# Row sums of the softmax weights with 128 moving columns instead of 4, in a recurrence followed by a soft mixture of experts

## The chip, the cores and the metric

The kernel runs on one core of one Trainium2 chip. The metric is the device time of one execution in microseconds; the figure given for a kernel is the median of several executions. A profile of one further execution shows what each engine did: TensorE (PE for its matmuls, PEld for its weight loads), VectorE (DVE), ScalarE (ACT), GpSimd (POOL) and SyncE (SP), which here only issues transfers.

## The reference

```
def _attn_ref(x, f_logit, lower_bound):          # 4 sequences of 5056 tokens, 256 channels
    sig = 1.0 / (1.0 + np.exp(-f_logit))
    f = lower_bound + (1.0 - lower_bound) * sig
    i = 1.0 - f
    for t in range(S):
        h = f[:, t] * h + i[:, t] * x[:, t]
        y[:, t] = h

def _moe_ref(x, phi, w1, w2):                    # all 20224 tokens; 8 experts of 4 slots, F = 1024
    logits = x @ phi                             # 32 slots
    d = softmax of logits over the tokens
    slot_input = d.T @ x
    for e in range(E):
        h = np.maximum(slot_input[e] @ w1[e], 0.0)
        slot_out[e] = h @ w2[e]
    c = softmax of logits over the slots
    return c @ slot_out
```

The output is 20224 x 256 in float32, 20.7 MB. The change is about the denominators of `c`: for each token the sum of its 32 exponentials.

## The kernel before

There are three stages.

*Recurrence.* Tokens come in 10 groups of 512 for each of the 4 sequences, 40 units in all. SyncE issues the loads of `x` and `f_logit`, ScalarE computes the gates, TensorE turns them to channels on partitions, VectorE runs the scans, TensorE turns the result back and multiplies it with `phi`. ScalarE writes the exponentials to `etall`, which stays on chip: 128 partitions (4 sequences x 32 slots) by 5056 tokens, bf16. The sums over the tokens, `slot_ps`, gather in PSUM along the way. GpSimd issues the loads of the expert weights (`load_w`); the last expert's `w2` comes in three parts.

*Experts.* After the last unit all is one chain on TensorE: slot inputs (L596), first layer (L624), transposes of its result (L639), second layer of the first four experts (L660) and then of the last four (L670), eight matmuls of 128x128 weights and 256 columns for each expert. Between those eight-matmul pieces lie the row sums: after the first of the four experts `row_sums(0)` with 16 matmuls, after the second `row_sums(1)` and `row_sums(2)` with 16 and 7, one small matmul for the 64 tokens left over (L393), and `SPINS = 7` matmuls whose results nobody reads (`spin`, L151, 256 columns each). The last two experts follow, then four more spins. VectorE takes the reciprocals of the sums (L677, L683, L684) into `rrow`, and scales the second layer's result to `slot_out` (L686); GpSimd makes `slot_bd` from it (L688).

*Output.* For every 128 tokens a matmul of the exponentials with `slot_out` (L705, one sequence, 32 weight rows) or `slot_bd` (L755, two sequences, 64 weight rows) gives the weighted sum, VectorE or ScalarE scales it by `rrow` while moving it out of PSUM (L695, L699 and L760, L766), and SyncE issues the store (L727 for the first 2 MB in small pieces, L769, L743, L786 afterwards).

The instruction order on each engine is the order of the program text. `row_sums` takes 128 tokens at a time as the weights of a matmul: the column `ew[:, :, r]` is a view of `etall` with a step of 16 elements (7 in the last block). The moving operand is `ones`, 128 partitions by 4 columns, column b being one on the 32 partitions of sequence b. So the result is 128 tokens by 4 sequences, and it goes to 4 neighbouring float32 columns of `rs_ps`, which is a view of the first half (one bank of 512 columns) of the PSUM tile `tail`. The second half of `tail` takes the spins' results. Columns 256 to 319 of the first half held the slot inputs, which were read long before.

Of the kernel before, what the change touches and what calls it, by code (L numbers as in the profile page):

```python
# [10 lines left out]
BF16 = mybir.dt.bfloat16  # L11
# [7 lines left out]
def kernel(  # L19
# [10 lines left out]
    nc = tc.nc  # L30
    B, S, D = x.shape
# [4 lines left out]
    P = 128  # L36
    DC = D // P
    FC = F // P
    R = 4
    G = P * R  # L40
    n_grp = (S + G - 1) // G
# [25 lines left out]
    consts = ctx.enter_context(tc.tile_pool(name="consts", bufs=1))  # L67
# [16 lines left out]
    def rep_constants(b):  # L84
        blk = ident_f[ds(b * NS, NS), ds(b * NS, NS)]
        nc.gpsimd.tensor_copy(rep[ds(b * NS, NS)], blk.unsqueeze(1).broadcast_to([NS, B, NS]))

    ones = consts.tile([P, B], BF16, name="ones")
    nc.vector.memset(ones, 0.0)
    for b in range(B):  # L90
        nc.vector.memset(ones[ds(b * NS, NS), ds(b, 1)], 1.0)

# [69 lines left out]
    with tc.tile_pool(name="sp2", bufs=3) as sp2, \  # L162
# [24 lines left out]
        def long(n):  # L187
            return 2 * B <= n < n_unit - 2 * B
# [38 lines left out]
        def gate(n, k=2):  # L227
            if n % 2 == 0:
                sts[n // 2] = sp2.tile([P, 2, R, D], BF16, name="s_t", tag="s_t")
            s_t, f_t = sts[n // 2][:, ds(n % 2, k)], fs[n // 2][:, ds(n % 2, k)]  # L230
            if n // B == odd:
                m = (R + R3) * D
                s_t = s_t.rearrange("p u r d -> p (u r d)")[:, :m]
                f_t = f_t.rearrange("p u r d -> p (u r d)")[:, :m]
            nc.scalar.activation(s_t, f_t, ACT.Sigmoid, scale=-1.0)  # L235
# [33 lines left out]
        def s_to_channels(n):  # L269
            if n % 2 == 0:  # L270
                pss[n // 2] = psp.tile([P, 2, P, R], F32, name="sp", tag="sp")
            to_channels(n, pss[n // 2][:, n % 2], sts[n // 2][:, n % 2],
                        sts[n // 2][:, 0, R3])
# [12 lines left out]
        def decay(n, k=2, os=range(DC)):  # L286
            T = used(n // B)
            sp = pss[n // 2].rearrange("c u p r -> c u (p r)").bitcast(BF16)
            if long(n):
                sp = sp.rearrange("c u (p r o) -> c p u r o", r=R, o=DC)  # L290
                for o in os:
                    decays[n // 2, o] = apool.tile([P, 2, G], F32, name="a", tag=f"a{o}")
                    a = decays[n // 2, o].rearrange("c u t -> c (u t)").rearrange(
                        "c (p u r) -> c p u r", u=2, r=R)
                    nc.scalar.activation(a, sp[:, :, :, :, o], ACT.Identity,  # L295
                                         scale=nomlb[:, ds(o, 1)], bias=1.0)
                return
            sp = sp.rearrange("c u (t o) -> c u t o", o=DC)
            for o in os:
                if n % 2 == 0:  # L300
                    decays[n // 2, o] = apool.tile([P, 2, G], F32, name="a", tag=f"a{o}")
                nc.scalar.activation(decays[n // 2, o][:, ds(n % 2, k), :T],  # L302
                                     sp[:, ds(n % 2, k), :T, o], ACT.Identity,
                                     scale=nomlb[:, ds(o, 1)], bias=1.0)
# [57 lines left out]
        def exps(g):  # L362
            gs = batch_of(g)
            if g == gs[-1]:
                T = sum(rows(i) for i in gs) * R
                nc.scalar.activation(etall[:, ds(first(gs[0]), T)], lgs[0][:, :T], ACT.Exp,
                                     accum_out=csum[:, ds(g, 1)])
# [16 lines left out]
                ets[k] = et[:, i]  # L384

        def row_sums(i):
            t0, n_r = blocks[i]
            ew = etall[:, ds(t0, P * n_r)].rearrange("s (p r) -> s p r", r=n_r)
            for r in range(n_r):
                nc.tensor.matmul(rs_ps[:, t0 // P + r], ew[:, :, r], ones,  # L390
                                 start=True, stop=True, skip_group_check=True)
            if i == len(blocks) - 1:
                nc.tensor.matmul(rs_ps[:, n_grp * R - 1, ds(0, B // 2)],  # L393
                                 left.rearrange("s t u -> s (t u)"), pair_ones,
                                 start=True, stop=True, skip_group_check=True)
# [17 lines left out]
        def unit(f, m):  # L413
            if 0 <= m < n_unit:
                f(m)
# [64 lines left out]
        for n in range(n_unit):  # L480
            if n < SINGLE - 2:
                if n:
                    unit(to_tokens, n - 1)
                    unit(u_to_channels, n + 1)
                s_to_channels(n + 2)
                if n + 3 < SINGLE:
                    gate(n + 3, 1)
                decay(n + 2, 1)
                if n + 3 == SINGLE:
                    gate(n + 3)  # L490
                if n % 2 == 0:
                    unit(load, n + AHEAD)
                unit(enter, n + 3)
                rep_constants(n)
            else:
                end = n >= n_unit - 6
                if n % 2 == 0:
                    unit(load, n + AHEAD)
                    if n == SINGLE - 2:
                        to_tokens(n - 1)  # L500
                        keep_tokens(n - 1)
                    if not end and n >= SETTLED:
                        unit(gate, n + 4)
                else:
                    unit(decay, n + 1)
                    if n < SETTLED:
                        gate(n + 3)
                    if n == n_unit - 5:
                        gate(n + 3)
                        exps(odd - 1)  # L510
                if not end and n != n_unit - 7:
                    group(exps, n - 2)

                unit(enter, n + 3)
                for _ in range(W_AT.get(n, 0)):
                    load_w(w_next[0])
                    w_next[0] += 1

                if n == n_unit - 2:
                    unit(u_to_channels, n + 1)  # L520
                if n != SINGLE - 2:
                    unit(to_tokens, n - 1)
                if n == n_unit - 2:
                    keep_tokens(n - 1)
                if n % 2 == 0:
                    unit(s_to_channels, n + 2)
                    unit(s_to_channels, n + 3)
                if n != n_unit - 2:
                    unit(u_to_channels, n + 1)
                if n in (n_unit - 5, n_unit - 4):  # L530
                    idle(2)
                elif n == SINGLE - 2:
                    idle(1, True)
                elif n < n_unit - 4 and n % (2 * B) in (1, 5, 6, 7):
                    idle(2 if n in (6, 7) else 1)
                if n == n_unit - 2:
                    tail = psp.tile([P, 2, G], F32, name="tail", tag="sp")
                    rs_ps = tail[:, 0, ds(0, n_grp * R * B)].rearrange(
                        "p (q b) -> p q b", b=B)
                    late_ps, odd_ps = (  # L540
                        tail[:, 1].bitcast(BF16)[:, ds(i * R * P, R * P)].rearrange(
                            "p (r s) -> p r s", r=R) for i in range(2))
                    logits(odd)
                    exps(odd)
                    slots(odd - 1)
                    spin(tail[:, 1], 1, G)
                    odd_weights()
                elif not end and long(n - 1):
                    if n % B == 0:
                        g = (n - 1) // (2 * B) * 2  # L550
                        for i in range(2):
                            logits(g + i, [2, 3] if n % (2 * B) == 0 else [0, 1])
                elif not end:
                    group(logits, n - 1)
            if n == n_unit - 1:
                logits(last, [0, 1, 2])
                late_exps([0, 1, 2])
                idle(1)
                late_weights([0, 1, 2], nc.scalar.copy)

            unit(scan, n)
            if n not in (SINGLE - 2, n_unit - 2):
                unit(keep_tokens, n - 1)
            if n == n_unit - 3:
                weights_to_tokens(odd - 1)
                slots(odd - 2)
            elif not n >= n_unit - 6:
                group(weights_to_tokens, n - 3)
                batch(slots, n - 4, 0)
                batch(slots, n - 4, 1)  # L570
                if n > 2 * B and n % (2 * B) == 3:
                    idle(1)
# [254 lines left out]
```

## Time and profile before

| | |
|---|---|
| median of 3 runs | 198.8 us (198.79 to 198.85) |
| the profiled execution | 199.45 us, of which the span shown is 197.7 us |
| PE, DVE, ACT, POOL busy | 78%, 73%, 70%, 52% of the span |
| mean granted TensorE clock | 0.862 |
| moved by DMA | 70.75 MB, mean 358 GB/s |
| recurrence, experts, output | to about 128 us, to 144.5 us, to 195 us |

The page cuts the span into 40 slices of 4.94 us. Its digits are tenths; PEclk is the clock that TensorE was granted, in tenths of full speed:

```profile
PE   0688599888989979897979888999969999960000
...
PEclk9999979999999999999999999999696555555555
DMA  5999999999999999999999999999639999999995
```

Slice 28 (counted from 0) begins at 138 us. Times in all other views count from the start of the span; a line such as "136.66 0.93 PE tail L390 x16" in the chain of waits says that from 136.66 us on, for 0.93 us, sixteen matmuls of line 390 into the tile `tail` were the work that everything behind them waited for.

### The profile page before, as it was taken

To read this page: it belongs to the slowest core of one execution; us is meant where nothing else is said; L and a number is where in the kernel's file an instruction comes from. 1 tells how busy PE (TensorE), PEld (TensorE's weight loads), DVE (VectorE), ACT (ScalarE), POOL (GpSimd) and SP (SyncE) were. 2 spreads that over 40 slices of the span, in tenths; PEclk is the share of its full clock that TensorE was granted. 3 is DMA by queue.
4 is the path that set the end of the run, shared out by engine and by line. 5 is a ranking of instruction groups with operands and counts; after the bars stand their busy time and mean duration, and the time that the engine had idled before them with its cause. 6 is when DMAs were issued, how large, how long until landed. Compare 5 with 4: busy or idle time off the path is not lost.

```text
span 197.7 us, 3232 instructions
## 1 busy us (share of the span) xinstructions
PE 153.2 (78%) x1198; PEld 107.1 (54%) x1198; DVE 143.6 (73%) x165; ACT 137.4 (70%) x193; POOL 103.1 (52%) x78
## 2 busy tenths in 40 slices
PE   0688599888989979897979888999969999960000
PEld 0477468675766758675766676558753533310000
DVE  2669779999899999999999999343168877850000
ACT  3588678899699998899996794621057889990000
POOL 2689586884998488895979886390030000000000
PEclk9999979999999999999999999999696555555555
DMA  5999999999999999999999999999639999999995
GB/s 209 417 420 422 427 431 423 428 426 347 390 426 428 380 356 423 426 409 306 411 421 354 264 219 213 215 212 212 107 119 423 419 421 424 428 458 438 424 424 215
DMA packets 14161, 70.75 MB, mean 358 GB/s; under 512 B 1585, under 2 KB 2866, under 8 KB 10178
## 3 DMA queue, kind: packets, MB, share of 16 engines
q1 hardware_dynamic: 11520, 62.13, 75.9%
q0 software_dynamic: 2624, 8.42, 21.4%
q8 instruction: 9, 0.15, 0.3%
q14 instruction: 6, 0.05, 0.1%
q10 hardware_dynamic: 2, 0.00, 0.0%
HBM read 58.23 MB, written 20.71 MB: 399 GB/s over the span
## 4 chain that ended last, share of the span: by engine, by line
PE 37%; DVE 23%; DMA 14%; POOL 6%; ACT 5%; issue 4%; SPq 0%; ACTq 0%; DVEq 0%; POOLq 0%
DVE h L313 16%; DMA x_t<-in_x_dram 14%; PE op L755 12%; POOL u_t L246 6%; DVE ht L343 4%; PE hp L326 3%; PE up L267 3%; PE so_ps L670 2%; PE sp L261 2%; PE op L705 2%; PE lg L357 2%; PE tail L151 2%; DVE ob L695 1%; PE slot_ps L407 1%; PE slot_ps L183 1%
## 5 line engine op out<-in xcount | busy, mean ns | idle before, releaser
L246 POOL TENSOR_TENSOR u_t<-s_t,x_t 128x1024 bf16<-128x1024 bf16 (+1 forms) x39 | 82.4, 2128 | 22.5 <-ACT s_t L235 14.0
L313 DVE TENSOR_TENSOR_SCAN h<-a,h,up 128x512 bf16<-128x512 f32 (+1 forms) x72 | 86.9, 1252 | 3.5 <-PE up L267 1.9
L235 ACT ACTIVATE s_t<-f_t 128x2048 bf16<-128x2048 f32 (+2 forms) x23 | 38.3, 1668 | 6.8 <-DMA f_t<-in_f_logit_dram 6.8
L326 PE MATMUL hp<-ident_f,h 128*128 128x128 f32 (+1 forms) x160 | 29.3, 308 | 7.7 <-DVE ht L343 5.9
L326 PEld LDWEIGHTS hp<-ident_f,h 128*128 128x128 f32 (+1 forms) x160 | 23.3, 207 | 17.9 <-DVE ht L343 11.3
L261 PE MATMUL sp<-ident_f,s_t 128*128 128x128 f32 x144 | 21.8, 296 | 6.3 <-ACT s_t L235 4.4
L295 ACT ACTIVATE a<-sp,lbs 128x1024 f32<-128x1024 bf16 x24 | 25.4, 1115 | 0.6 <-PE sp L261 0.6
L755 PE MATMUL op<-slot_bd,etall 64*128 64x512 bf16 x62 | 24.1, 594 | 1.7 <-DVE ob L695 1.4
L766 ACT ACTIVATE oc<-op,rrow 128x256 f32<-128x256 f32 x60 | 22.7, 489 | 2.8 <-PE op L755 2.3
L760 DVE TENSOR_TENSOR oc<-op,rrow 128x1024 f32<-128x1024 f32 x16 | 19.2, 1222 | 5.3 <-PE op L755 5.3
L261 PEld LDWEIGHTS sp<-ident_f,s_t 128*128 128x128 f32 x144 | 17.5, 151 | 8.2 <-ACT s_t L235 5.3
L302 ACT ACTIVATE a<-sp,lbs 128x512 f32<-128x512 bf16 (+2 forms) x22 | 17.8, 858 | 4.2 <-PE sp L261 3.8
L267 PE MATMUL up<-ident_f,u_t 64*128 64x64 f32 x192 | 17.8, 230 | 2.0 <-POOL u_t L246 1.8
L183 PE MATMUL slot_ps<-rep,ident_f 128*128 128x256 f32 x54 | 17.7, 423 | 0.1
L755 PEld LDWEIGHTS <-etall 64*128 64x128 bf16 x62 | 8.9, 154 | 15.5 <-issue 11.7
L267 PEld LDWEIGHTS up<-ident_f,u_t 64*128 64x128 f32 x192 | 14.0, 138 | 6.0 <-POOL u_t L246 2.5
L343 DVE COPY ht<-hp 128x512 f32<-128x512 f32 (+1 forms) x22 | 14.7, 669 | 1.2 <-PE hp L326 1.2
L343 ACT COPY ht<-hp 128x512 f32<-128x512 f32 (+1 forms) x18 | 10.5, 581 | 6.7 <-PE hp L326 6.7
L699 ACT ACTIVATE ob<-op,rrow 128x256 f32<-128x256 f32 x15 | 5.8, 477 | 10.9 <-PE op L705 10.7
L313 DVE TENSOR_TENSOR_SCAN h<-a,up 128x512 bf16<-128x512 f32 x8 | 9.3, 1209 | 2.6 <-ACT a L302 1.8
L261 PE MATMUL up<-ident_f,u_t 128*128 128x128 f32 x48 | 9.8, 338 | 0.7 <-POOL u_t L246 0.7
L183 PEld LDWEIGHTS slot_ps<-rep,ident_f 128*128 128x128 f32 x54 | 8.6, 193 | 2.5 <-issue 1.1
(107 smaller groups left out, 152.5 us busy)
## 6 DMA issues: line engine op xcount, KB each, us to landing
f_t<-in_f_logit_dram SPq DMA_DIRECT2D x12, 1024.0 KB, 12.5
x_t<-in_x_dram SPq DMA_DIRECT2D x12, 1024.0 KB, 12.1
out_dram<-oc SPq DMA_DIRECT2D x6, 2048.0 KB, 11.1
w_sb<-in_moe_w_dram POOLq DMA_DIRECT2D x14, 512.0 KB, 10.9
f_t<-in_f_logit_dram SPq DMA_DIRECT2D x12, 512.0 KB, 8.4
x_t<-in_x_dram SPq DMA_DIRECT2D x12, 512.0 KB, 9.9
out_dram<-oc SPq DMA_DIRECT2D x4, 896.0 KB, 5.2
out_dram<-ob SPq DMA_DIRECT2D x1, 2048.0 KB, 8.2
```

The source lines that it names most:

```text
L183: nc.tensor.matmul(slot_bank[:, 1], ident_f, wide_rep, start=False, stop=False, skip_group_check=True)
L235: nc.scalar.activation(s_t, f_t, ACT.Sigmoid, scale=-1.0)
L246: nc.gpsimd.tensor_tensor(uts[n][:, :r], s_t[:, :r], x_t[:, :r], ALU.mult)
L261: nc.tensor.transpose(ps[:, :, r], t[:, r], ident_f)
L267: nc.tensor.transpose(v[:, :, r], t(r)[k].bitcast(F32), ident_f[k, k])
L295: nc.scalar.activation(a, sp[:, :, :, :, o], ACT.Identity, scale=nomlb[:, ds(o, 1)], bias=1.0)
L313: nc.vector.tensor_tensor_scan(h[:, :T, o], decays[n // 2, o][:, n % 2, :T], up[:, :T, o], hs[number(g - 1, b)][:, ds(used(g - 1) - 1, 1), ...
L326: nc.tensor.transpose(hp[:n_p, r], hw[:, :n_p, r], ident_f)
L343: copy(hts[g][:n_p, b].rearrange("p r d -> p (r d)").bitcast(F32), hps.pop(n)[:n_p].rearrange("p r c -> p (r c)"))
L755: nc.tensor.matmul(op[:, i_r].rearrange("p u d -> p (u d)"), ew[:, :, r + i_r], slot_bd[ds(j * 2 * NS, 2 * NS)].rearrange("s u d -> s (u d)"),
L760: nc.vector.tensor_tensor(ob[:, :, ds(r, k)].rearrange("p u r d -> p r u d"), op[:, ds(0, k)], scale[:, ds(r, k)].unsqueeze(3).broadcast_t ...
L766: nc.scalar.activation(ob[:, u, r + i_r], op[:, i_r, u], ACT.Copy, scale=scale[:, r + i_r, ds(u, 1)])
```

## The change

`ones` becomes 128 x 128. Its first four columns are as before, the other 124 are ones. Each of the 39 matmuls of `row_sums` streams all 128 columns and so writes 128 float32 columns, from the column at which its own four begin. The next matmul, four columns further, overwrites all but the first four of these, and so on; what lies to the right of the last matmul's four columns is read by nobody. The line numbers below `ones` move by one; the blank line in `row_sums` moves those behind it by another, and `sums` by a third.

```
-    ones = consts.tile([P, B], BF16, name="ones")
-    nc.vector.memset(ones, 0.0)
+    ones = consts.tile([P, P], BF16, name="ones")
+    nc.vector.memset(ones, 1.0)
+    nc.vector.memset(ones[:, ds(0, B)], 0.0)
     for b in range(B):
         nc.vector.memset(ones[ds(b * NS, NS), ds(b, 1)], 1.0)
...
         def row_sums(i):
+
             t0, n_r = blocks[i]
             ew = etall[:, ds(t0, P * n_r)].rearrange("s (p r) -> s p r", r=n_r)
             for r in range(n_r):
-                nc.tensor.matmul(rs_ps[:, t0 // P + r], ew[:, :, r], ones,
+                nc.tensor.matmul(sums[:, ds((t0 // P + r) * B, P)], ew[:, :, r], ones,
                                  start=True, stop=True, skip_group_check=True)
...
                     tail = psp.tile([P, 2, G], F32, name="tail", tag="sp")
-                    rs_ps = tail[:, 0, ds(0, n_grp * R * B)].rearrange(
+                    sums = tail[:, 0]
+                    rs_ps = sums[:, ds(0, n_grp * R * B)].rearrange(
                         "p (q b) -> p q b", b=B)
```

## The prediction

> **What bounds the kernel now.** I read the shares of the page first, then the chain of waits of the last third, then the granted clock in stretches, then the start of the output stage. Two stages matter. From 148 us on the output transfers set the time: the DMA share is about 1 until 195 us (0.92 to 1.22 over stretches of 2 us), at about 425 GB/s for 20.7 MB, while the last computing instruction ends at 178 us. So whatever brings the first output forward brings the end forward, as long as the transfers then stay fed. Before that, between the last scan and the first output, the weights for the output are a chain of TensorE work without a gap. Its pieces (start, length, both in us, engine, tile, line, count):
>
> ```profile
> 136.23 0.43 PE so_ps L674 x2
> 136.66 0.93 PE tail L390 x16
> 137.60 0.89 PE so_ps L670 x8
> 138.49 1.30 PE tail L390 x23
> 139.79 0.03 PE tail L393
> 139.82 1.42 PE tail L151 x7
> 141.24 2.79 PE so_ps L670 x16
> 144.03 0.03 issue
> 144.06 0.49 DVE slot_out L686
> ```
>
> The 39 row sums (L390) are on the path: 58 ns each in the first block (0.93/16), 57 ns in the second (1.30/23). The line L670 shows what else happens: eight of its matmuls took 0.89 us (111 ns each), and the next sixteen 2.79 us (174 ns each), with the same shape. The stretches tell why. They are cut 3.41 us apart, at the points where the granted clock changes; the columns are stretch, length, busy time of PE, PEld, DVE, ACT and POOL with counts, granted clock, DMA share, GB/s:
>
> ```profile
> 17.02:20.44 3.42, 2.39 (x17) 1.68 (x15) 3.42 (x5) 2.60 (x4) 3.28 (x3) 1.00 1.02 419
> 20.44:23.85 3.41, 1.43 (x10) 1.24 (x11) 2.57 (x4) 2.67 (x3) 1.15 (x3) 0.99 1.04 432
> 23.85:27.26 3.41, 3.29 (x16) 2.13 (x18) 2.23 (x3) 2.61 (x3) 3.27 (x3) 0.51 1.02 432
> ...
> 136.44:139.85 3.41, 3.41 (x52) 3.25 (x50) 0.56 (x1) 0.00 (x0) 0.00 (x0) 0.99 1.08 207
> 139.85:143.27 3.42, 3.42 (x18) 2.36 (x17) 0.76 (x2) 0.00 (x0) 0.00 (x0) 0.51 0.40 67
> 143.27:146.68 3.41, 3.15 (x27) 2.54 (x25) 2.14 (x5) 1.56 (x5) 1.83 (x2) 1.00 0.08 27
> 146.68:150.09 3.41, 1.81 (x8) 0.95 (x9) 2.56 (x4) 2.09 (x7) 0.00 (x0) 0.99 0.97 371
> 150.09:153.51 3.42, 3.42 (x10) 1.11 (x10) 2.94 (x3) 3.01 (x9) 0.00 (x0) 0.50 1.02 423
> ```
>
> The clock falls to 0.50 three times, always at the end of a stretch in which TensorE did little: 1.43 of 3.41 us busy before 23.85, 1.81 before 150.09. Stretches with 2.37 us (68.16 to 71.58) or 2.39 us keep it. From 23.85 to 139.85 are 34 periods of 3.412 us: the stretches follow a fixed beat. The stretch before the middle fall, 136.44 to 139.85, is the row sums. It looks 100% busy, but a busy PE in this view is instructions in flight. The work in it is eight matmuls of 256 columns (0.89 us) and 39 of 4 columns. Counting a column at 111/256 = 0.43 ns, 0.89 us for the first plus 39 x 4 x 0.43 ns = 0.07 us, and about 0.2 us of L674, make 1.2 of 3.41 us: less than in either of the other stretches that ended in a fall.
>
> The Trainium skill ("TensorE: Matmul & The Clock Gate", Part 1) has the same beat, a free-running window of 3,413 ns, and the same two clocks; here the dips last 3.41 us. But it ties the throttle to idle windows and busy-ness, and in this window PE had no idle time at all. By its rule of no idle gaps above some 3 us the row sums would be innocent, wide ones would change nothing there, and the time would stay near 199. The row above, which falls after a window that is full of instructions and nearly empty of columns, decides against that reading.
>
> **The change part by part.** *Setup.* One more memset, and a larger one, at the start on DVE. The present one (L89) took 60 ns at 0.79 us and those behind it end by 2.03 us; DVE then waits 0.39 us for the identity (L82) and 2.53 us for the first x_t (L242). About 0.1 us more goes into the first wait; without that cover it would cost 0.1 us. Nothing in it: 0.
>
> *The row sums.* Each of the 39 matmuls streams 128 columns instead of 4, behind the same 128x128 weight load. No trace row has this exact form with an f32 result. The nearest are transposes with bf16 weights and 128 bf16 columns, one of which reads the same tile etall:
>
> ```profile
> L378 PE MATMUL ep<-ident,etall x32: 218/220/247, 42.5 to 118.8; 128*128 128x128 bf16 x32
> ...
> L639 PE MATMUL ht_ps<-ident,hi x16: 223/224/253, 132.7 to 134.0; 128*128 128x128 bf16 x16
> ...
> L390 PE MATMUL tail<-ones,etall x39: 168/201/204, 136.5 to 139.6; 128*128 128x4 bf16 x39
> ```
>
> Eight of L378 lie within 0.60 and 0.64 us, so they start (0.60 - 0.22)/7 = 55 to 60 ns apart; eight of L639 within 0.67 and 0.69 us, 64 to 67 ns apart. The columns hide behind the next weight load. I take 61.5 ns, between the two, against 57 now: 39 x 4.5 = +0.17 us (-0.08 at 55, +0.38 at 67). The far bound is no overlap at all: 57 ns for the load plus 128 columns at 0.43 ns makes 112, 39 x 55 = +2.15 us.
>
> The same page ("Back-to-back issue gap") speaks against the change: it gives about 81 ns for each load-and-matmul pair of 128 columns in a sustained stream. By that the row sums would cost 39 x 24 = +0.94 us, an estimate, and the sum below would end near 198.6 instead of 197.9. The rows of L378 and L639 lie below that figure.
>
> *The clock after them.* With 128 columns the window to 139.85 holds some 0.2 us of L674, 0.89 of L670 and, for the row sums, at 55 ns of columns in every 61.5, 2.1 us: 3.2 of 3.41. That is above every window that kept the clock, so it stays at 1.00 until 143.27. Seven spins then cost 7 x 111 = 0.78 instead of 1.42 us (-0.64), the sixteen of L670 1.78 instead of 2.79 (-1.01). Nothing else may be late: the last four weight transfers landed at 139.4 (120.9 + 18.5), 140.7 (122.5 + 18.2), 141.4 (125.0 + 16.4) and 142.1 (127.5 + 14.6), and I have PE at their matmuls at 140.8, 141.7, 142.1 and 142.3. The last has 0.2 us to spare. VectorE's reciprocals (0.73 and 0.11 us behind the spins) end before 142 and are wanted after 143. Sum: +0.17 - 0.64 - 1.01 = -1.48 us; slot_out starts at 142.6 instead of 144.06.
>
> *What is given back.* Output work now reaches 1.5 us further into the beat. The window 143.27 to 146.68 loses the full matmuls of its first 1.2 us and holds only sixteen of L705 (256 columns on 32 rows, 16 x 111 = 1.8 us at most) and the first of L755. The window 146.68 to 150.09, with eight of 512 columns on 64 rows (1.7 us of columns), ended in a fall, so this one should as well, and the clock drops at 146.68 instead of 150.09. The first output weights of L755 then run at half clock. How the transfers stand there now:
>
> ```profile
> 145.58 3.34 SPq L727 DMA_DIRECT2D out_dram<-ob  x7
> ...
> 148.22 1.24 PE L755 MATMUL op<-slot_bd,etall 64*128 64x512 bf16 x5
> ...
> 149.12 1.20 ACT L766 ACTIVATE oc<-op,rrow 128x256 f32<-128x256 f32 x3 [1.32 <-PE op L755]
> ...
> 151.13 0.83 SPq L769 DMA_DIRECT2D out_dram<-oc  x2
> ```
>
> L727 issues 2 MB. Adding up the GB/s from 146.0, 0.37 MB of it are left at 151.0, which are gone at 151.9; the first transfer of L769, issued at 151.13, needs 0.5 us or more before it moves data (L727's: 145.58 to 146.1). So there is no slack. Matmuls of L755 start 215 ns apart now; at half clock 430. The fourth one, for which ACT's first activation waits, comes 3 x 215 = 0.65 us later, and ACT paces that transfer (six activations of 0.36 us behind each other). I take +0.6 us of empty DMA, which nothing makes up later, since the transfers are the bound to the end. Ends: 0 (the clock holds, or the transfers run on) and +0.9 (two more half-clock matmuls in front). Total -1.48 + 0.6 = -0.9 us.
>
> The profiled execution took 199.45 us, 197.7 of span and 1.75 around it; the median of the runs is 198.8. All terms are differences within the span, so I put them on the median: **197.9 us**.
>
> **The rivals.** (1) *Nothing is given back*: the window to 146.68 passes as busy. For it: PE would be in flight some 2.0 of 3.4 us there, and it lies between the windows that fell (1.81) and that held (2.37). Against: 32-row matmuls, while 160 to 170 us, 10.00 of 10.00 us busy with 64-row ones, never wins the clock back. Time 198.8 - 1.48 = 197.3, chance 0.20. (2) *The wide matmul pays part of its columns*, 70 to 95 ns: 39 x 13 to 38 = 0.5 to 1.5 us in place of 0.17. With the same giveback 198.2 to 199.1, say 198.5; chance 0.09. L378 speaks against it; the step between weight columns speaks for it (16 elements in L390, 4 in L378, and the loads took 165 against 113 ns). (3) *The change doesn't do it*: the clock falls at 139.85 regardless, because the monitor counts something else than columns, or timed runs have another beat than the profiled one. Then only +0.17 is left, 199.0, chance 0.11. Three runs within 0.06 us speak against a beat that wanders. (4) *Slower*: load and columns don't overlap for these strided weights, 112 ns. Row sums end 2.15 us later; the gain of 1.65 is used up at 57 + 1.65/0.039 = 99 ns. If the clock is kept this gives 198.8 + 2.15 - 1.65 = 199.3; since PE would then stream only half of the time, the fall may come as well and the time is 200.9. Chance 0.10. The forecast itself keeps 0.50.
>
> **How the numbers follow.** The likeliest case is 197.9, with its own range of 197.6 to 198.5 from the terms' ends. Rival 1 takes the range down to 197.1, rival 2 up to 198.9; what is left out is rival 4 and part of rival 3, under 0.2. No change means within 0.2%, 0.4 us, which is about what a measurement of this kernel can tell. Faster: forecast, rival 1 and most of rival 2, 0.76. Same: most of rival 3 and a part of 2, 0.14. Slower: rival 4, 0.10.
>
> **What would show it.** Row sums 55 to 67 ns apart in the chain; granted clock 1.00 from 139.85 to 143.27; spins and L670 at 111 ns; slot_out at 142.6; then a fall at 146.68, the first issue of L769 near 150.3 and a notch in the DMA share behind the 2 MB. I am wrong if the clock still falls at 139.85, if the row sums lie 80 ns or more apart, or if L670 waits for its last weights.

## The result and the profile after

The changed kernel takes 200.44 us in the median (200.06 to 201.38), the kernel before 198.89 us on the same chip; the ratio is 1.0071, with a 95% interval of 1.0046 to 1.0096. The forecast was 197.9, in a range of 197.1 to 198.9. The change makes the kernel slower, by 0.7%. Executions more than 1.5% above the fastest of their kernel (one each of e1, e3, e4 and e10 below) are left out of the ratios.

The profiled execution is the slowest of the six, 201.38 us with a span of 199.6 us. The chain of waits of the changed kernel, from the first layer to the output weights (start, length, engine, tile, line, count; its lines stand up to three lower in the text of the kernel):

```profile
133.06 2.10 PE hi_ps L627 x31
...
139.11 0.99 PE tail L392 x16
140.10 0.87 PE so_ps L673 x8
140.97 1.38 PE tail L392 x23
...
142.36 0.79 PE tail L152 x7
143.15 1.76 PE so_ps L673 x16
...
144.93 0.06 DVE slot_out L689
```

Inside the experts stage the lengths are those of the forecast: row sums 62 and 60 ns apart, seven spins in 0.79 us, the sixteen matmuls of the last two experts in 1.76 us instead of 2.79. From the first layer to slot_out it takes 11.87 us instead of 13.45. Whether the change brought these lengths is another matter: kernels with 4 columns show them too, in the section on the columns. And the first layer itself starts at 133.06 us; before, it started at 130.61 us. The 2.45 us were lost in the recurrence, for which the forecast had only one term, the setup at 0. They compare one execution with one: in the profile of e6 below, whose load buffers stay where they were, the first layer starts at 132.97 us. So a part of the 2.45 us can be the spread of executions.

The stretches of the beat, and behind them three half microseconds of the output (stretch, length, busy time of PE, PEld, DVE, ACT, POOL, granted clock, DMA share, GB/s), for the changed kernel:

```profile
141.30:144.71 3.41, 3.41 (x42) 3.15 (x41) 0.76 (x2) 0.00 (x0) 0.00 (x0) 1.00 0.39 65
144.71:148.12 3.41, 2.58 (x22) 2.04 (x20) 2.71 (x6) 2.12 (x6) 1.83 (x2) 1.00 0.24 77
148.12:151.53 3.41, 2.67 (x8) 1.06 (x9) 1.82 (x2) 1.26 (x4) 0.00 (x0) 0.50 1.02 384
152.50:153.00 0.50, 0.50 (x2) 0.23 (x2) 0.50 (x2) 0.50 (x2) 0.00 (x0) 0.50 0.88 336
153.00:153.50 0.50, 0.50 (x3) 0.23 (x2) 0.50 (x1) 0.13 (x2) 0.00 (x0) 0.50 0.01 0
153.50:154.00 0.50, 0.50 (x2) 0.15 (x1) 0.49 (x1) 0.50 (x2) 0.00 (x0) 0.50 0.56 229
```

The clock holds through the experts and falls at 148.12, 3.2 us behind slot_out (6.0 us before). The notch in the transfers, a gap between the first 2 MB and the next large transfer, is there: a share of 0.01 and 0.56, some 0.8 us of empty DMA with what is missing at 152.5. From slot_out to the end of the span it takes 54.67 us instead of 53.62. The profiled execution adds up: +2.45 - 1.58 + 1.05 = +1.92 us, and the spans are 197.7 and 199.6.

What happened to the loads shows in a stretch during them. The kernel before:

```profile
10.00:35.00 25.00, 21.14 (x122) 17.01 (x123) 20.84 (x22) 19.92 (x22) 19.00 (x14) 0.93 1.02 425
```

The changed kernel:

```profile
10.00:35.00 25.00, 18.95 (x124) 15.32 (x124) 21.36 (x22) 20.09 (x22) 18.87 (x13) 1.00 1.02 414
```

The DMA engines are busy all the time in both (share 1.02), and move 425 and 414 GB/s. The packets themselves got longer: those of 8 KB, which fill the load buffers, take 310.9 ns in the mean before and 314.6 after, the 4 KB ones of the loads in this stretch 159.0 and 163.1; those of 16 KB, which empty the output buffers, 612.2 and 617.2. The whole queue of loads and stores, before and then changed (packets, MB, share of the span of 16 engines):

```profile
q1 hardware_dynamic: 11520, 62.13, 75.9%
q1 hardware_dynamic: 11520, 62.13, 76.4%
```

The same packets and bytes took 150.0 us of each DMA engine's time before and 152.5 us in the changed kernel.

Nothing in the change touches a transfer, except that `ones` grew from 8 to 256 bytes in each partition. Places are handed out one behind the other in steps of 32 bytes, so everything allocated after `ones` lies 224 bytes further:

```
tile     before                     after                      (byte in the partition)
ones     19232                      19232
etall    19328                      19552
w1_sb0   32256                      32480
f_t      89600, 97792, 105984       89824, 98016, 106208
x_t      114176, 122368, 130560     114400, 122592, 130784
ob       32256, 48640, 65024        32480, 48864, 65248
```

The load and output buffers lay at multiples of 512 bytes, and lie at 224 past a multiple of 256 now.

### The profile page after: what moved, and what is told of

The parts are those of the page before. It is cut to its first block, busy times and chain, and to the rows that moved or that the text cites. A ratio compares the mean times of both kernels' runs of the same rounds, so it can differ in the third digit from the quotient of the medians.

```text
span 199.6 us, 3233 instructions
## 1 busy us (share of the span) xinstructions
PE 152.1 (76%) x1198; PEld 106.2 (53%) x1198; DVE 144.0 (72%) x166; ACT 138.0 (69%) x193; POOL 103.2 (52%) x78
## 4 chain that ended last, share of the span: by engine, by line
PE 39%; DMA 21%; DVE 19%; issue 4%; POOL 3%; ACT 2%; ACTq 0%; SPq 0%; DVEq 0%; POOLq 0%
DMA x_t<-in_x_dram 14%; DVE h L314 13%; PE op L758 12%; DMA f_t<-in_f_logit_dram 7%; PE hp L327 4%; PE up L268 4%; DVE ht L344 3%; POOL u_t L247 3%; PE sp L262 3%; PE lg L358 2%; PE so_ps L673 2%; PE op L708 2%; PE slot_ps L184 2%; DVE ob L698 1%; ACT oc L769 1%
## 5 line engine op out<-in xcount | busy, mean ns | idle before, releaser
L314 DVE TENSOR_TENSOR_SCAN h<-a,h,up 128x512 bf16<-128x512 f32 (+1 forms) x72 | 86.9, 1252 | 5.4 <-PE up L268 4.2
L758 PE MATMUL op<-slot_bd,etall 64*128 64x512 bf16 x62 | 25.0, 622 | 1.6 <-DVE ob L698 1.4
L262 PEld LDWEIGHTS sp<-ident_f,s_t 128*128 128x128 f32 x144 | 18.0, 154 | 9.3 <-ACT s_t L236 5.5
L268 PEld LDWEIGHTS up<-ident_f,u_t 64*128 64x128 f32 x192 | 14.2, 140 | 6.9 <-POOL u_t L247 3.3
L358 PE MATMUL lg<-h,phi 128*32 128x512 bf16 (+1 forms) x80 | 9.6, 389 | 0.0
```

The lines of the kernel that those rows point to most:

```text
L262: nc.tensor.transpose(ps[:, :, r], t[:, r], ident_f)
L268: nc.tensor.transpose(v[:, :, r], t(r)[k].bitcast(F32), ident_f[k, k])
L314: nc.vector.tensor_tensor_scan(h[:, :T, o], decays[n // 2, o][:, n % 2, :T], up[:, :T, o], hs[number(g - 1, b)][:, ds(used(g - 1) - 1, 1), ...
L758: nc.tensor.matmul(op[:, i_r].rearrange("p u d -> p (u d)"), ew[:, :, r + i_r], slot_bd[ds(j * 2 * NS, 2 * NS)].rearrange("s u d -> s (u d)"),
```

## Experiments

Three theories: the addresses (the wide tile pushed the transfers' buffers off a boundary), the columns (the 124 further ones cost something that the forecast missed), and an accident of the clock's beat or of the chip. All twelve kernels are compared with the kernel before on the same chip; the median of the latter was 199.41, 198.90 and 199.18 us in the three groups.

### The addresses without the columns, and the columns without the addresses

`e1_layout_only`, from the kernel before:

```
-    ones = consts.tile([P, B], BF16, name="ones")
+    ones = consts.tile([P, P], BF16, name="ones")[:, :B]
```

> The kernel before, with the tile ones allocated 128 columns wide, of which only the first four are set and used: the row sums stream 4 columns as before, but every tile that is allocated after ones lies 224 bytes further, at 32 past a multiple of 64 bytes. Theory of the addresses (the change lost time because the wider ones moved the big buffers): no gain in the experts stage, the whole loss of the changed kernel: about 2.4 us later at the first layer and 0.5 to 0.8 us more in the output, 201.5 (200.5 to 202.3), with 8 KB load packets at 313 ns instead of 309. Rival, the loss comes from the 124 further columns: 198.9, packets at 309. Rival, the loss is an accident of the beat of the clock or of the chip: 198.9 here too.

`e2_columns_only`, from the changed kernel:

```
-    PAD = 160
+    PAD = 48
```

> The changed kernel, with the unused padding behind etall cut by 112 elements (224 bytes), so that all tiles behind etall lie where they lay in the kernel before; etall itself stays 224 bytes further. Theory of the addresses: first layer starts at the time of the kernel before, the gain of the experts stage (1.5 us) less the notch in the output transfers (0.6 to 0.9 us) is left: 198.0 (197.4 to 198.4), packets at 309 ns. Rival, the columns lose the time: 200.4 as the changed kernel. Rival, accident: anything between 198 and 200.4, not repeated over the rounds.

e1 measured 1.0083 (1.0044 to 1.0122), the whole loss of the change, with 4 columns streaming. e2 measured 0.9988 (0.9956 to 1.0019). Packets of 8 KB: 314.5 ns in e1, 310.9 in e2. The loss follows the addresses and not the columns. But e2 is 198.97 in the median, not 198.0: the gain that was to be left over is hardly there, which the section on the columns takes up.

### Which distance

`e3_shift32`, `e4_shift64`, `e7_shift256` and `e12_shift128` are the kernel before with `PAD` at 176, 192, 288 and 224 in place of 160, and nothing else. All tiles behind `etall` lie 32, 64, 256 and 128 bytes further.

> The kernel before with 16 more elements (32 bytes) of padding behind etall and nothing else: ones, etall and the row sums as before, all later tiles 32 bytes further. Theory of the addresses, in the form that 32 past a multiple of 64 is what costs: as slow as e1, 201.5 (200.5 to 202.3). If instead the 224 bytes or the place of etall mattered: 198.9. Rival of the columns or accident: 198.9.

> The kernel before with 32 more elements (64 bytes) of padding: all later tiles at a multiple of 64 bytes again, but no longer of 512. Theory of the addresses, multiples of 64: 198.9 as before, packets at 309 ns. If multiples of 512 are what counts: slow as e1, 200.5 or more. Rival of the columns or accident: 198.9.

> The kernel before with 256 more bytes of padding behind etall: all later buffers at multiples of 256, not of 512. If the grain is 512 bytes: slower by 0.4 to 0.8% with packets spread from 309 to 321 ns. If it is 128 or 256 bytes: as before, all packets at 309.

> The kernel before with 128 more bytes of padding: all later buffers at multiples of 128, not of 256. Multiples of 256 were as fast as those of 512, multiples of 64 alone 0.48% slower. If the grain is 256 bytes: slower by 0.3 to 0.6%, load packets of 8 KB spread from 309 to 320 ns. If it is 128: as before, all at 309.

With the kernels of the other sections (mean packet times in ns, from the packets of the profiled execution; fastest: the fastest of all its executions, for the changed kernel one more than the six of its median):

| kernel | columns | load / output buffers | 8 KB load | 16 KB store | ratio to before | fastest, us |
|---|---|---|---|---|---|---|
| before | 4 | 512 / 512 | 310.9 | 612.2 | 1 | 197.88 |
| changed | 128 | +224 / +224 | 314.6 | 617.2 | 1.0071 (1.0046 to 1.0096) | 199.79 |
| e1_layout_only | 4 | +224 / +224 | 314.5 | 617.2 | 1.0083 (1.0044 to 1.0122) | 199.91 |
| e3_shift32 | 4 | +32 / +32 | 314.5 | 617.1 | 1.0067 (1.0036 to 1.0098) | 199.86 |
| e4_shift64 | 4 | +64 / +64 | 313.6 | 617.1 | 1.0048 (1.0014 to 1.0081) | 199.60 |
| e12_shift128 | 4 | +128 / +128 | 312.9 | 617.1 | 1.0095 (1.0063 to 1.0127) | 199.44 |
| e7_shift256 | 4 | +256 / +256 | 310.8 | 612.2 | 0.9984 (0.9957 to 1.0010) | 197.83 |
| e5_loads_only | 4 | +32 / 512 | 314.5 | 611.9 | 1.0043 (1.0013 to 1.0072) | 199.42 |
| e6_stores_only | 4 | 512 / +32 | 310.8 | 617.0 | 1.0002 (0.9972 to 1.0031) | 198.15 |
| e2_columns_only | 128 | 512 / 512 | 310.9 | 612.2 | 0.9988 (0.9956 to 1.0019) | 198.04 |
| e9_columns_in_pad | 128 | 512 / 512 | 310.8 | 612.1 | 0.9994 (0.9967 to 1.0020) | 198.02 |

The grain is 256 bytes: 32, 64 and 128 are slow, 256 is as fast as 512. The fastest executions of the kernels in this table part without overlap, 197.83 to 198.15 with the load buffers on multiples of 256 and 199.42 to 199.91 off them. The form of the theory that blamed 32 past a multiple of 64 fell with e4.

The Trainium skill has a rule that fits ("DMA: Bandwidth & Descriptors", "How a descriptor splits into AXI transactions"): transactions of 256 bytes start at multiples of 256, and a descriptor that doesn't start there fetches what lies in front of it too. The grain agrees with the runs, in which the moved side is the one that loads write and stores read. The price does not follow the wasted bytes: by the rule a start at 224 would cost seven 32-byte beats more than the 256 of 8 KB, 2.7%, and a start at 32 one, 0.4%, an estimate from that page; here 314.6 and 314.5 ns, 1.2% for both.

### Loads or stores

`e5_loads_only` puts 32 unused bytes in front of the load buffers, `e6_stores_only` in front of the output buffers, both in the kernel before:

```
+    shim = held.enter_context(tc.tile_pool(name="shim", bufs=1))
+    shim.tile([P, 16], BF16, name="shim")
     ld = held.enter_context(tc.tile_pool(name="ld", bufs=3))
```

```
-    with tc.tile_pool(name="osb", bufs=3) as osb:
+    with tc.tile_pool(name="shim", bufs=1) as shim, \
+         tc.tile_pool(name="osb", bufs=3) as osb:
+        shim.tile([P, 16], BF16, name="shim")
```

> The kernel before with 32 unused bytes in front of the load buffers: f_t and x_t and the working buffers of the recurrence lie 32 bytes further, the weights, etall and the output buffers where they were. So far: all later buffers 32 bytes further cost 0.67%, 64 bytes 0.48%, the wide ones without their columns 0.83%. Theory that the transfers are what suffers, each at its own buffers: load packets of 8 KB at 313 ns, store packets of 16 KB still at 611; the loads are 41 of the 62 MB on that queue, and the recurrence waits for them, so most of the loss, 0.3 to 0.7%. Rival, the stores alone matter: no difference. Rival, compute buffers matter: a loss, but with load packets at 309 and longer instructions.

> The kernel before with 32 unused bytes in front of the output buffers only (ob, oc). Theory of the transfers: store packets of 16 KB at 615 ns instead of 611 and 7 KB ones at 276 instead of 272, load packets at 309; the stores set the time for 48 us, at some 1% of them 0.3 to 0.5 us, 0.15 to 0.3%. Rival, the loads alone matter: no difference.

Each moved its own packets and no others, as the table shows. The same stretch of the loads in e5:

```profile
10.00:35.00 25.00, 20.55 (x118) 16.48 (x118) 20.04 (x21) 19.31 (x22) 18.85 (x13) 0.86 1.02 415
```

and in e6:

```profile
10.00:35.00 25.00, 20.48 (x117) 16.34 (x117) 19.90 (x20) 18.62 (x23) 20.15 (x13) 0.86 1.02 424
```

Both have the same mean clock in this stretch (0.86) and the same number of matmuls within one; the rate differs, 415 against 424. All kernels of the table divide like this: 424 or 425 GB/s with the load buffers on multiples of 256 (before, e2, e6, e7, e9), 414 to 416 off them (changed, e1, e3, e4, e5, e12), on either side at clocks from 0.86 to 1.00. e5 moves the working buffers of the recurrence too, but the instructions on them keep their lengths: 2128 ns before and 2130 in e5 for GpSimd's products (L246 of the kernel before), 1252 in both for VectorE's scans (L313), 1668 in both for ScalarE's gates (L235). So it is the transfers that suffer. The loads carry the measurable part: 1.0043. The stores' packets are 0.8% longer, which over 48 us would be 0.4 us; 1.0002 with its interval can neither show nor exclude that.

### The columns alone, and the clock

`e9_columns_in_pad` keeps every address of the kernel before, that of `etall` too, by setting the wide ones into the unused padding:

```
-    ones = consts.tile([P, P], BF16, name="ones")
...
+    consts.tile([P, B], BF16, name="ones")
...
+    etpad = store.tile([P, S + PAD], BF16, name="etall")
+    etall, ones = etpad[:, :S], etpad[:, ds(S + PAD - P, P)]
```

> The changed kernel with its 128 wide ones placed in the unused padding behind etall: every other tile, etall too, lies where it lies in the kernel before, so this is the change of the columns and nothing else. Theory: the wide columns keep the clock where the beat would have let it fall at the row sums, which the profiles show in one of seven executions with 4 columns, so the mean gain is 1.5/7 = 0.2 us less the notches of the output: 0.997 to 1.000 of the kernel before, packets at 309 ns, no execution with spins at half clock. Rival, the gain is in every execution: 0.992 to 0.996. Rival, the columns cost something of their own: above 1.002.

0.9994 (0.9967 to 1.0020): no difference that can be told. In the profiles the reason is plain. Eight kernels with single 4-column row sums were profiled (before, e1, e3, e4, e5, e6, e7, e12), and only one of them, the kernel before, shows the fall at the row sums. The chain of e4, with 4 columns:

```profile
139.11 0.94 PE tail L390 x16
140.05 0.89 PE so_ps L670 x8
140.94 1.30 PE tail L390 x23
...
142.27 0.79 PE tail L151 x7
143.06 1.76 PE so_ps L670 x16
```

The spins and the last two experts take as long as in the changed kernel, and from the first layer to slot_out e4 takes 11.78 us, the changed kernel 11.87. None of the four with 128 columns (changed, e2, e8, e9) shows the fall either. The beat lies differently in each execution: the first rise of the clock stands at 16.93 us in the profile of before and between 14.2 and 16.9 us in the others.

To make the result independent of where the beat lies, `e10_narrow_thrice` (from the kernel before) and `e11_wide_thrice` (from e2) compute the second and third block of row sums three times over, so that the stretch of row sums is longer than a beat:

```
-            for r in range(n_r):
+            for r in [*range(n_r)] * (3 if i else 1):
```

> The kernel before with the second and third block of row sums computed three times over: 46 more matmuls of 4 columns, 2.6 us at 57 ns, so that the stretch with few columns (3.9 us) is longer than a beat of 3.41 us wherever the beat lies. Theory that few columns let the clock fall: a fall in nearly every execution, 3.41 us at half clock, of which 1.4 to 1.7 us are lost: 198.9 + 2.6 + 1.3 = 202.8 (202.2 to 203.4). Rival, the fall before was not due to the columns: 201.5, no fall near the row sums.

> The changed kernel with the later buffers at their old addresses and the second and third block of row sums three times over: 46 more matmuls of 128 columns, 2.8 us at 60 ns. Theory: the clock is kept until the output stage in every execution, 198.7 + 2.8 = 201.5 (201.0 to 202.0), and 0.8 to 1.6 us less than with 4 columns three times over, although each matmul is slower. Rival, the columns don't matter to the clock: 0.2 to 0.4 us more than with 4 columns three times over.

Measured: 1.0342 (1.0295 to 1.0388) with 4 columns, 206.32 us, and 1.0242 (1.0196 to 1.0289) with 128, 203.94 us. The wide ones are 2.4 us faster, more than the 0.8 to 1.6 us expected; both kernels take longer than expected, e10 by 3.5 us and e11 by 2.4. The chain of e10 and three of its stretches:

```profile
140.09 4.03 PE tail L390 x69
...
144.14 1.52 PE tail L151 x7
145.65 3.41 PE so_ps L670 x16
```

```profile
139.51:142.92 3.41, 3.41 (x56) 3.38 (x54) 0.28 (x1) 0.00 (x0) 0.00 (x0) 1.00 0.48 79
142.92:146.33 3.41, 3.41 (x36) 2.72 (x35) 0.64 (x1) 0.00 (x0) 0.00 (x0) 0.50 0.00 0
146.33:149.75 3.42, 3.42 (x17) 2.24 (x15) 0.60 (x3) 0.00 (x0) 0.00 (x0) 0.50 0.00 0
```

The same of e11:

```profile
138.78 4.17 PE tail L392 x69
...
142.95 0.79 PE tail L152 x7
143.74 1.76 PE so_ps L673 x16
```

```profile
138.87:142.28 3.41, 3.41 (x59) 3.41 (x58) 0.00 (x0) 0.00 (x0) 0.00 (x0) 1.00 0.72 124
142.28:145.70 3.42, 3.42 (x40) 3.06 (x38) 0.93 (x3) 0.00 (x0) 0.00 (x0) 1.00 0.00 0
```

In both a whole beat is full of instructions, 3.41 of 3.41 us busy. Behind the one with narrow matmuls the clock falls, here for two beats, and the 23 matmuls behind it take 4.93 instead of 2.55 us; behind the one with wide matmuls it holds. So columns, not instructions in flight, keep the clock. The difference of the two lies where it should: from the first layer to slot_out e10 takes 16.9 us and e11 14.67, and from slot_out to the end of the span 56.0 and 55.78.

What missed is the level of both. The row sums of e11 cost the 2.8 us that were expected (14.67 us, against 11.88 in e9), but its 55.78 us behind slot_out are 53.74 in e9. A notch in the transfers accounts for about 1 us of that: the first large transfer is issued 8.01 us behind slot_out, 7.26 in e9, and the DMA share from 153.5 to 154.0 us is 0.00. The other 1 us is at the end: from 198.2 to 199.6 us there is only one packet under way at a time, in e9 for 0.3 us. e10 ends in the same way. Both load a tenth 16 KB of instructions during the output (at 174.6 us in e11, 0.88 us long), where all other kernels load nine, the last before 146 us; that this is what holds up the last packets is not shown. The clock of e10 stayed low for two beats where the expectation had one.

### The notch

`e8_columns_split` cuts the first pair of large output transfers in two, in e2 (`early` is set for this pair only):

```
+                if early and t == 1:
+                    for u in range(2):
+                        nc.sync.dma_start(out=rows_of(i, 2 * j + u)[:, ds(0, 4)],
+                                          in_=ob[:, u, ds(0, 4)])
+            q = ds(4, n_r - 4) if early else ds(0, n_r)
             for u in range(2):
-                nc.sync.dma_start(out=rows_of(i, 2 * j + u), in_=ob[:, u])
+                nc.sync.dma_start(out=rows_of(i, 2 * j + u)[:, q], in_=ob[:, u, q])
```

> The changed kernel with the later buffers at their old addresses (as in e2) and the first pair of output transfers (896 KB each) cut in two, the first four of seven rows issued as soon as they are scaled. Theory: the notch in the output transfers, where the clock has fallen by the time of the first output weights, is filled, so it beats e2 (0.9988) by up to 0.4%: 0.995 to 0.998 of the kernel before. Rival, the notch doesn't decide or the smaller transfers cost as much: 0.999 as e2 or above.

0.9999 (0.9966 to 1.0031): no gain. In its profile the clock had fallen 2.9 us behind slot_out, and the lowest share of DMA at that place is 0.79 in one half microsecond (0.68 in another, 3.5 us later), so the notch was mostly filled; what that is worth lies below what these runs can tell. No version was found that beats the kernel before by more than its interval.

## Why the prediction was wrong

**The bounds** were right as far as they went: the changed kernel is limited by the transfers in the output stage, and by the chain on TensorE between the last scan and slot_out. The loads of the recurrence, with a DMA share of 1.02 from 10 to 35 us, were not among them, and it is there that the change lost.

**The setup** is the first step that failed. The forecast priced the larger tile by its memset, "Nothing in it: 0". The memset is indeed free: 165 ns instead of 60, and the cast of the identity behind it starts at 2.42 us in both. The tile's size is not: it moved every later buffer by 224 bytes, and the packets that fill the load buffers became 1.2% longer in a stage in which DMA is busy without a gap. e1 shows that this alone costs 0.83%, 1.7 us, which is the sign and the size of the result; e2 and e9 show that without it no loss is left. None of the rivals had this. The slower one, weight loads and columns that don't overlap, was not what happened; that its 200.9 lies near the 200.44 is chance.

**The clock** is the second, in the step from one profile to the median. The mechanism stands: e10 falls behind narrow matmuls and e11 holds behind wide ones. But the changed kernel's profile does not show it. Its beat turned at 141.30 us, in the middle of the second block of row sums and not at its end as before, and e4 shows that an execution with 4 columns can have the same short spins and experts. That -1.58 us from the first layer to slot_out lies so near the forecast of -1.48 is luck: the profile of the kernel before had the fall, and the other seven with 4 columns do not. "Three runs within 0.06 us speak against a beat that wanders" was wrong: 29 later executions of the same kernel, those beside e1 to e4, spread from 197.88 to 200.68 us, and one profile in eight shows the fall. At 1.5 us in one of eight executions the gain is 0.2 us in the mean, an estimate from few profiles; e9 measures -0.1 us, between -0.7 and +0.4. The part of rival 3 that doubted the beat should have had far more than its share of 0.11. Together, 1.7 us for the addresses and -0.1 for the columns make the 1.5 us by which the medians differ; the forecast had 0 and -0.9.

**The row sums** were sized well: 62 and 60 ns apart, 61.5 forecast. The 81 ns of the Trainium skill ("TensorE: Matmul & The Clock Gate", "Back-to-back issue gap"), weighed against the rows of L378 and L639, did not apply, and rival 2 is out.

**The notch** came, larger than forecast: first issue of L772 at 152.94, 8.01 us behind slot_out instead of 7.07, and then empty DMA; from slot_out to the end 1.05 us more, where the forecast had 0.6 and at most 0.9. But it is not a price of the change. e1 and e3, with 4 columns, have it too (8.02 us in both), because their clock fell 2.4 and 3.3 us behind slot_out; e2, with 128, does not (7.08 us; the clock fell after 5.1). Where the beat lies decides. Some of the 1.05 us may belong to the longer packets of the stores: e4 and e12, with the clock as late as before, need 53.9 us behind slot_out where the kernel before needs 53.6.

## What to carry to other kernels

A constant that grows moves whatever is allocated behind it: before pricing an edit by its instructions, compare the places of the transfers' buffers before and after, and keep them on multiples of 256 bytes (a wide constant can go behind them, or into padding). A stall that shows in one profile and hangs on a free-running beat is worth its length times the share of executions that have it; one execution, or three that agree, do not give that share.

## What the hardware showed unexpectedly

Off the 256-byte boundary the packets are not only longer but spread: of the 8 KB ones nine in ten took at most 309 ns before, and at most 321 ns in the changed kernel. The cost depends little on how far the start is off: 314.5 ns at 32 bytes and at 224, 313.6 at 64 and 312.9 at 128. Why is open. The weights' transfers, which go through another queue and change the type on the way, did not notice the shift: their 4 KB packets have a median of 322 ns in all of these kernels in the first 100 us, where their buffers moved and where they did not.

In the output stage of the kernel before PE is 10.00 of 10.00 us busy from 160 to 170 us and the clock stays at 0.50, with matmuls that use 64 of the 128 weight rows; whether the number of rows counts for the clock as the columns do is not shown.
